# Keeping layer B's weighed sums with features on partitions, and spreading their denominators through memory

## The chip, the cores and the metric

The kernel runs on one core of a Trainium2 chip, in one launch. The metric is the device time of an execution in microseconds; the time of a kernel is the median of its executions.

## The reference, cut to what matters

Four layers, A, B, A, B, each with a residual, over x of 2048 x 640 with 32 heads of 20 features. Layer A is linear attention. Layer B cuts the sequence into four segments of 512 and adds, by a gate for each head, an exact attention inside the segment and a read of a memory of the segments before it:

```python
for s in range(N):
    qs, ks, vs = q[:, :, s], k[:, :, s], v[:, :, s]
    logits = jnp.einsum("bhqd,bhkd->bhqk", qs, ks) * scale + mask
    p = _softmax(logits, axis=-1)
    a_dot = jnp.einsum("bhqk,bhkd->bhqd", p, vs)
    pq = phi(qs)
    num = jnp.einsum("bhld,bhde->bhle", pq, M)
    den = jnp.einsum("bhld,bhd->bhl", pq, z)[..., None] + 1e-6
    a_mem = num / den
    o = g * a_mem + (1.0 - g) * a_dot
    outs.append(o)
    ...
return o @ wo
```

In segment 0 the memory is empty, so a_mem is 0 there. The change is in the division of the exact attention by the softmax's sum, and in what follows it up to the product with wo.

## The kernel before, in words

Two streams of work are woven into one program. `dense` makes the projections, layer A, the memory reads and the output products. `attention` makes layer B's exact attention in 64 groups: two layers, four segments, eight groups of four heads. `run` takes a step from whichever stream has the lower sum of estimated costs; a step of attention counts SLOT (2420 ns), and three steps (the three stretches of STRETCHES) make one round. TensorE (PE) executes in the order so written; the instructions of the other engines and of SP's queue are put in order by the framework's scheduler.

Three groups are in work in a round. The new group gets its queries and keys from memory by four transfers on SP (`stacks`; the tiles qs and ks). `row_max` multiplies queries by keys and takes each query's maximum on VectorE (DVE) in five portions. `split_max` makes two halves of the maxima (the tile m, L1022 and L1023), `max_rows` turns them on PE (L1031), copies them on ScalarE (ACT; the tile mt, L1033), and stores them by two SP transfers as two more rows of the queries (L1036). Then `scores` can multiply keys by queries with the maximum already taken off (L1048), ACT takes the exponential (L1052), GpSimd (POOL) masks it (L1059), and `weigh` multiplies it with the values (L1075). The values carry a column of ones, so PSUM holds, for each of four heads, 20 rows of weighed sums and one row of denominators, at 32 partitions a head, over 512 queries on the free dimension.

`evacuate` copies this to SBUF (oTf, L1081), with the denominator scaled by the gate. In the next stretch `normalize` turns it by four fp32 transposes on PE (L1088), so that tokens are on partitions; DVE takes the reciprocals of the denominators (L1091) and multiplies (L1098; L1095 in segment 0), and POOL adds the product to the memory's part, which lies in the tile otok (L1099). `b_memory` has written that part. `b_out` makes the output: for each tile of 128 tokens, five fp32 transposes back to features on partitions (`turn`, L319), a split in two fp16 halves by ACT (L323) and DVE (L324), and two half products with wo (`o_half`, L395), the residual by ACT and POOL (L476, L477).

In the first layer B, `b_out` of segment s - 2 is woven into the projections of segment s, and those of segments 2 and 3 into the next layer A. In the second, the four run at the end, beside the attention of segment 3, and segments 0 and 1 wait for that in memory (`b_spill`). SP's queue, in order, carries the loads of queries and keys, the stores of the projections (L859 to L863), the rows of the maxima, and the loads of x and of layer A's queries. PSUM is handed out in rotation, eight banks.

Of the kernel before, what the change touches and what calls it, by code (L numbers as in the profile page):

```python
# [142 lines left out]
class Kernel:  # L143
# [18 lines left out]
    def setup(self):  # L162
# [7 lines left out]
        self.g_last = cp.tile([P, D + 1], F32, name="g_last")  # L170
# [351 lines left out]
    def g_first(self, s, box, w, L, behind=None):  # L522
# [30 lines left out]
        def memory():  # L553
            if s == 0:
                L["v"] = [self.new_v(None) for _ in range(C - 1)]
                L["G"] = [v[:, :D + 1] for v in L["v"]] + [self.g_last]
# [308 lines left out]
    def b_project(self, st):  # L865
# [68 lines left out]
    def b_memory(self, st, mem):  # L934
        st["o"] = self.sb.tile([P, NT, D], F32, tag="big", name="otok", bufs=3)
        if st["s"] > 0:
            for i in range(NT):
# [4 lines left out]
    def b_spill(self, st):  # L942

        od = self.dr.tile([NT, P, D], F32, name="od%d" % st["s"])
        self.nc.sync.dma_start(od.rearrange("i p d -> p i d"), st["o"])
        st["od"], st["o"] = od, None
        yield 0.0

    def b_out(self, st, wo, src, dst, norm):

        yield lambda: st.get("attended")
# [4 lines left out]
        def turned(i):  # L956
            if st["o"] is not None:
                o = st["o"][:, i]
            else:
                o = self.row("ol")  # L960
                nc.sync.dma_start(o, st["od"][i])
            oT.append(self.new_oT())
            return self.turn(o, oT[i], 0)
# [3 lines left out]
        for i in range(NT):  # L967
# [3 lines left out]
            for n in range(2):  # L971
                yield from (c for c in [next(t, None)] if c)
                self.o_half(oT[i], wo, "B", x, xn, n, later=not st.get("ends"))
# [105 lines left out]
    def evacuate(self, G):  # L1079
        G["oT"] = self.bp.tile([P, 512], F32, tag="oTf", name="oTf", bufs=1)  # L1080
        self.nc.scalar.activation(G["oT"], G["pv"], AF.Copy, scale=self.cg[:, G["g"]:G["g"] + 1])  # L1081

    def normalize(self, G):
        nc, bp, sb, g, st = self.nc, self.bp, self.sb, G["g"], G["st"]
        oT = G["oT"]
# [4 lines left out]
        rc = sb.tile([P, NT, 4], F32, tag="rc4", name="rc4", bufs=2)  # L1090
        nc.vector.reciprocal(rc, pr[:, :, :, DH])  # L1091
        o = st["o"][:, :, 80 * g:80 * g + 80].rearrange("q i (h e) -> q i h e", h=4)
        rb = rc[:, :, :, None].to_broadcast([P, NT, 4, DH])
        if st["s"] == 0:
            nc.vector.tensor_tensor(o, pr[:, :, :, :DH], rb, op=OP.mult)  # L1095
        else:
            tmp = sb.tile([P, NT, 4, DH], F32, tag="er", name="tmp", bufs=3)
            nc.vector.tensor_tensor(tmp, pr[:, :, :, :DH], rb, op=OP.mult)  # L1098
# [264 lines left out]
```

## Time and profile before

| | |
|---|---|
| median of 3 executions | 1738.13 us (1735.6 to 1741.74) |
| the profiled execution | 1736.07 us, span 1734.4 us |
| granted TensorE clock | 0.998 |
| PE busy | 1666.1 us, 96% |
| DVE busy | 1180.9 us, 68% |
| ACT busy | 969.7 us, 56% |
| POOL busy | 517.7 us, 30% |
| moved by DMA | 187.58 MB, 108 GB/s on average |

The span is the time from the first to the last instruction of the profiled execution. An engine's busy time leaves out the issuing of transfers and waits on semaphores. A line of the groups reads: source line, engine, operation, out<-in by the program's tile names, shapes and count, then busy time in all and the mean of one in ns, then the idle time ahead of these instructions and what ended it. In the timeline the columns are start, duration, engine, line, operation. SPq is SP's queue issuing a transfer; its duration is the issue, not the transfer.

### The profile page before, as it was taken

What the parts mean: (1) busy time and instruction counts of PE and PEld (TensorE: products, weight loads), DVE (VectorE), ACT (ScalarE), POOL (GpSimd) and SP (SyncE); (2) the same over time, 40 slices, a digit from 0 to 9 for tenths busy, and PEclk for the clock granted to TensorE, in tenths of its full rate; (3) what the DMA queues carried; (4) which work ended last, traced back from release to release, by engine and by line L of the source; (5) the groups of instructions that cost most, each with busy time, mean ns of one, the idle gap of its engine ahead of it and who ended that gap; (6) DMA issues with size and microseconds to landing.
All of it is one profiled execution on the core that took longest, in us unless ns stands there. A gap on an engine that the chain in (4) does not pass through costs nothing.

```text
span 1734.4 us, 36014 instructions
## 1 busy us (share of the span) xinstructions
PE 1666.1 (96%) x13032; PEld 1047.5 (60%) x13032; DVE 1180.9 (68%) x3849; ACT 969.7 (56%) x1818; POOL 517.7 (30%) x982
## 2 busy tenths in 40 slices
PE   6999999999999999999999999999999999999998
PEld 4676667664565576556556777666546545645555
DVE  8645534577787677759864456746777877878773
ACT  5545433357557645667675544333665576666673
POOL 1543350012123312334351301221422432233452
PEclk9999999999999999999999999999999999999999
DMA  7522452422322322352211303423232323223432
GB/s 262 184 109 95 150 195 97 139 76 82 113 71 73 113 96 68 120 179 95 78 48 51 103 32 122 175 98 116 75 102 85 112 81 108 93 82 111 131 115 92
DMA packets 118330, 187.58 MB, mean 108 GB/s; under 512 B 13949, under 2 KB 79613, under 8 KB 115849
## 3 DMA queue, kind: packets, MB, share of 16 engines
q1 hardware_dynamic: 105896, 142.68, 25.5%
q0 software_dynamic: 3040, 21.63, 3.4%
q10 hardware_dynamic: 9216, 20.98, 3.1%
q8 instruction: 103, 1.69, 0.4%
q14 instruction: 75, 0.61, 0.1%
HBM read 106.05 MB, written 78.64 MB: 106 GB/s over the span
## 4 chain that ended last, share of the span: by engine, by line
PE 78%; DVE 10%; ACT 6%; issue 2%; POOL 2%; DMA 1%; SPq 1%; ACTq 0%; POOLq 0%; DVEq 0%
PE ps L395 32%; PE ps L381 17%; PE ps L1075 7%; PE ps L1048 4%; ACT pe L1052 3%; PE ps L1007 3%; PE ps L319 3%; PE ps L564 3%; PE ps L450 3%; DVE ps L1013 2%; PE ps L1088 1%; PE ps L891 1%; PE ps L730 1%; DVE st L338 1%; DVE xn L479 1%
## 5 line engine op out<-in xcount | busy, mean ns | idle before, releaser
L1013 DVE CUSTOM_DVE_ANT_0 ps<-ps,maskw 128x512 f32<-128x512 f32 (+3 forms) x1024 | 472.5, 519 | 38.0 <-PE ps L1007 35.7
L1052 ACT ACTIVATE pe<-ps,lsc 128x512 f32<-128x512 f32 x640 | 394.8, 696 | 87.6 <-PE ps L1048 84.9
L1059 POOL TENSOR_SCALAR_AFFINE_SELECT pe<-pe 128x256 f32<-128x256 f32 (+1 forms) x640 | 229.7, 365 | 449.2 <-ACT pe L1052 444.0
L395 PEld LDWEIGHTS <-xT 128*128 128x128 f16 x2880 | 280.3, 98 | 114.6 <-issue 9.3
L395 PEld LDWEIGHTS <-oT 128*128 128x128 f16 x1920 | 185.7, 98 | 80.5 <-issue 7.0
L1075 PE MATMUL ps<-pe,v 128*32 128x512 f32 (+3 forms) x2048 | 162.2, 436 | 11.5 <-POOL pe L1059 5.1
L395 PE MATMUL ps<-w_Bo,oT 128*128 128x320 f16 x960 | 142.3, 302 | 2.8 <-ACT pe L1052 1.1
L1013 DVE DVE_READ_ACCUMULATOR2_ANT mg<- 128x1 f32 x1024 | 143.9, 141 | 0.0
L381 PE MATMUL ps<-xT,w_Bq 128*128 128x512 f16 x600 | 140.2, 380 | 1.9 <-ACT pe L1052 0.8
L395 PE MATMUL ps<-w_Bv,xT 128*128 128x320 f16 x960 | 139.7, 300 | 0.8 <-DVE otok L1095 0.6
L381 PE MATMUL ps<-xT,w_Bk 128*128 128x512 f16 x600 | 138.8, 380 | 1.2 <-ACT pe L1052 1.2
L395 PE MATMUL ps<-w_Ak,xT 128*128 128x320 f16 x960 | 136.1, 300 | 0.0
L1007 PE MATMUL ps<-ks,qs 60*128 60x512 f16 (+3 forms) x1024 | 123.1, 298 | 6.7 <-ACT pe L1052 2.9
L856 DVE SCALAR_TENSOR_TENSOR nat<-ps,nat 128x512 f16<-128x512 f32 x80 | 55.2, 690 | 89.2 <-ACT nat L855 89.1
L1048 PE MATMUL ps<-qs,ks 62*128 62x512 f16 (+3 forms) x1024 | 105.9, 301 | 3.0 <-DMA qs<-mt 1.5
L1075 PEld LDWEIGHTS ps<-pe,v 128*32 128x32 f32 x2048 | 65.3, 109 | 71.9 <-issue 45.8
L421 POOL TENSOR_SCALAR e<-e 128x320 f32<-128x320 f32 (+1 forms) x52 | 82.9, 1594 | 82.4 <-ACT e L417 78.2
L855 ACT ACTIVATE nat<-ps 128x512 f16<-128x512 f32 x80 | 48.2, 603 | 91.8 <-PE ps L381 69.2
L381 PEld LDWEIGHTS <-w_Bk 128*128 128x128 f16 x600 | 57.3, 98 | 65.5 <-issue 5.6
L381 PEld LDWEIGHTS <-w_Bq 128*128 128x128 f16 x600 | 56.7, 98 | 65.9 <-issue 7.8
L1007 PEld LDWEIGHTS <-qs 60*128 60x128 f16 x1024 | 50.0, 94 | 70.9 <-issue 44.7
L343 POOL TENSOR_TENSOR rs<-rs,mhalf 128x1 f32<-128x1 f32 x48 | 27.0, 563 | 218.8 <-DVE rs L342 218.7
(217 smaller groups left out, 2630.7 us busy)
## 6 DMA issues: line engine op xcount, KB each, us to landing
x<-xn ACTq DMA_DIRECT2D x48, 320.0 KB
qs<-qd SPq DMA_DIRECT2D x128, 120.0 KB
ks<-kd SPq DMA_DIRECT2D x128, 120.0 KB
xo<-x SPq DMA_DIRECT2D x48, 320.0 KB
pqi<-pqd SPq DMA_DIRECT2D x32, 320.0 KB
qd<-nat SPq DMA_DIRECT2D x40, 256.0 KB
kd<-nat SPq DMA_DIRECT2D x40, 256.0 KB
x<-in_A_x SPq DMA_DIRECT2D x16, 320.0 KB
```

What stands on the lines that cost most here:

```text
L319: nc.tensor.transpose(pt[:, (c - c0) * P:(c - c0 + 1) * P], src[:, c * P:(c + 1) * P], self.ident)
L381: nc.tensor.matmul(p, w[:, c, a, t * P:(t + 1) * P], xT[:, c, b, :], start=k == 0, stop=k == 3 * C - 1)
L395: nc.tensor.matmul(p, xT[:, c, a, i * P:(i + 1) * P], w[:, c, b, n * HN:(n + 1) * HN], start=k == 0, stop=k == 3 * C - 1)
L421: nc.gpsimd.tensor_scalar(e, e, 1.0, eps, op0=OP.min, op1=OP.add)
L450: nc.tensor.matmul(nd[:, lo - k * cut:hi - k * cut], pq[t], mem[:, OFF[t] + lo - a:OFF[t] + hi - a], start=first, stop=True, skip_group_ch ...
L856: nc.vector.scalar_tensor_tensor(nat[:, 1], p, QK_SHIFT, nat[:, 0], op0=OP.mult, op1=OP.subtract)
L1007: nc.tensor.matmul(bs[par][:, a:a + n], qs[r, p, i * P:(i + 1) * P], ks[r, p, :n], start=True, stop=True)
L1013: nc.vector.tensor_tensor_reduce(bs[par][:, a:a + n], bs[par][:, a:a + n], self.maskw[:, SEG - n:], 1.0, NEG, OP.add, OP.max, G["mg"][:, p ...
L1048: nc.tensor.matmul(b[:, a:a + n], ks[r, p, j * P:(j + 1) * P], qs[r, p, j * P:], start=True, stop=True)
L1052: nc.scalar.activation(e, b, AF.Exp, scale=self.lsc)
L1059: nc.gpsimd.affine_select(d, d, pattern=pat, compare_op=OP.is_ge, fill=0.0, base=0, channel_multiplier=-1)
L1075: nc.tensor.matmul(G["pv"][32 * h4:32 * h4 + 32, j * P:], v[j][:, h * E1:h * E1 + 32], G.pop((p, par, j)), start=j == 0, stop=j == 2, skip ...
```

## The change

In all segments but the last of the second layer B, the weighed sums are not turned. `evacuate` stores the four rows of denominators to memory and loads them again, spread over 128 partitions x 16. `normalize` takes the reciprocals of these, stores them, loads each head's row 32 times over by four transfers (rb), multiplies oTf by rb in place on DVE, and packs the four heads' 20 rows each into od in memory, with features as rows, by four more transfers. Thus a group makes eleven more transfers, all on SP's queue. `merged` loads a tile of 128 tokens from od with features on partitions (ot). In segment 0 ACT and POOL split it at once; in the others PE turns the memory's part, DVE adds the two, and ACT and POOL split the sum. The last segment of the second layer B keeps the old way (`normalize_direct`). An output may start one round later than before (`packed` for `attended`).

```diff
-        self.g_last = cp.tile([P, D + 1], F32, name="g_last")
...
+                last = sb.tile([P, MW], F32, tag="mem", name="g_last", bufs=2)
+                L["G"] = [v[:, :D + 1] for v in L["v"] + [last]]
...
+        st["od"] = self.dr.tile([D, SEG], F32, tag="od", name="od", bufs=NSEG)
...
+    def merged(self, st, i, dst):
+        nc = self.nc
+        ot = self.row("ot").rearrange("p (c t) -> p c t", c=C)
+        nc.sync.dma_start(ot, st["od"].rearrange("(c p) t -> p c t", p=P)[:, :, i * P:(i + 1) * P])
+        if st["s"] == 0:
+            nc.scalar.activation(dst[:, :, 0], ot, AF.Copy)
+            nc.gpsimd.tensor_tensor(dst[:, :, 1], ot, dst[:, :, 0], op=OP.subtract)
+            return
+        if st["o"] is not None:
+            o = st["o"][:, i]
+        else:
+            o = self.row("ol")
+            nc.sync.dma_start(o, st["am"][i])
+        for c0, c1 in ((0, 3), (3, 5)):
+            pt = self.bank()
+            n = c1 - c0
+            for c in range(c0, c1):
+                nc.tensor.transpose(pt[:, (c - c0) * P:(c - c0 + 1) * P], o[:, c * P:(c + 1) * P], self.ident)
+            v = ot[:, c0:c1]
+            nc.vector.tensor_tensor(v, pt[:, :n * P].rearrange("p (c t) -> p c t", c=n), v, op=OP.add)
+            nc.scalar.activation(dst[:, c0:c1, 0], v, AF.Copy)
+            nc.gpsimd.tensor_tensor(dst[:, c0:c1, 1], v, dst[:, c0:c1, 0], op=OP.subtract)
+            yield n * 110.0
...
     def b_out(self, st, wo, src, dst, norm):
-        yield lambda: st.get("attended")
+        yield lambda: st.get("packed")
...
             oT.append(self.new_oT())
-            return self.turn(o, oT[i], 0)
+            return self.turn(st["o"][:, i], oT[i], 0) if st["direct"] else self.merged(st, i, oT[i])
...
     def evacuate(self, G):
-        G["oT"] = self.bp.tile([P, 512], F32, tag="oTf", name="oTf", bufs=1)
-        self.nc.scalar.activation(G["oT"], G["pv"], AF.Copy, scale=self.cg[:, G["g"]:G["g"] + 1])
+        nc, bp = self.nc, self.bp
+        G["oT"] = bp.tile([P, SEG], F32, tag="oTf", name="oTf", bufs=2)
+        nc.scalar.activation(G["oT"], G["pv"], AF.Copy, scale=self.cg[:, G["g"]:G["g"] + 1])
+        if G["g"] == NG - 1:
+            G["st"]["attended"] = True
+        if G["st"]["direct"]:
+            return
+        den = self.dr.tile([4, SEG], F32, tag="den", name="den", bufs=2)
+        nc.sync.dma_start(den, G["oT"][DH::32])
+        G["rd"] = bp.tile([P, 16], F32, tag="rd", name="rd", bufs=2)
+        nc.sync.dma_start(G["rd"], den.rearrange("h (q t) -> (h q) t", t=16))
 
     def normalize(self, G):
+        if G["st"]["direct"]:
+            return self.normalize_direct(G)
+        nc, g, st, oT, rd = self.nc, G["g"], G["st"], G["oT"], G["rd"]
+        nc.vector.reciprocal(rd, rd)
+        rden = self.dr.tile([4, SEG], F32, tag="rden", name="rden", bufs=2)
+        nc.sync.dma_start(rden.rearrange("h (q t) -> (h q) t", t=16), rd)
+        rb = self.sb.tile([P, SEG], F32, tag="er", name="rb", bufs=3)
+        for h in range(4):
+            nc.sync.dma_start(rb[32 * h:32 * h + 32], rden[h:h + 1].to_broadcast([32, SEG]))
+        nc.vector.tensor_tensor(oT, oT, rb, op=OP.mult)
+        for h in range(4):
+            r = 80 * g + DH * h
+            nc.sync.dma_start(st["od"][r:r + DH], oT[32 * h:32 * h + DH])
...
     def attention(self, segs):
...
+            if done and done["g"] == NG - 1:
+                done["st"]["packed"] = True
+            done = None if old and old["st"]["direct"] else old
             old, prev = prev, new
...
-            segs = [dict(s=s, w=wB, v=[], pq=[], acc=acc) for s in range(NSEG)]
+            segs = [dict(s=s, w=wB, v=[], pq=[], acc=acc, direct=last and s == NSEG - 1) for s in range(NSEG)]
...
-                    aux = chain(aux, when(segs[s - 2], "attended", late))
+                    aux = chain(aux, when(segs[s - 2], "remembered" if last else "packed", late))
```

How the instructions stand now, at two places. First SP's queue in the first layer B, segment 2, from one group's rows of maxima (qs<-mt) to the next group's; before:

```order
L1036 DMA qs<-mt 2x8x128 x2
L993 DMA qs<-qd 60x2x512 x2
L993 DMA ks_2752<-kd 60x2x512 x2
L330 DMA xo<-x_87 128x640
L1036 DMA qs<-mt 2x8x128 x2
```

and now, from the denominators of one group to the second row transfer of the next maxima (den, rd, rden and rb are the denominators and their reciprocals on their way, od the packed heads):

```order
L1111 DMA den<-oTf 4x512
L1016 DMA qs<-qd 60x2x512 x2
L1016 DMA ks_2751<-kd 60x2x512
L1113 DMA rd<-den 128x16
L1016 DMA ks_2751<-kd 60x2x512
L329 DMA xo<-x_86 128x640
L956 DMA ot<-od 128x5x128
L1123 DMA rden<-rd 128x16
L1126 DMA rb<-rden 32x512 x4
L1059 DMA qs<-mt 2x8x128
L1130 DMA od<-oTf 20x512 x4
L1059 DMA qs<-mt 2x8x128
```

The four packing transfers stand between the two row transfers of the next maxima. They stand so in 17 of the 56 changed groups; in 18 both row transfers come ahead of them, in 19 both come after, and in the last two of the first layer B no rows follow.

Then DVE at the same place. Before, the reciprocal and the product follow at once on PE's transposes, ahead of the rest of the maxima (L1013, printed as ISA, each with its readout):

```order
L1091 RECIPROCAL rc_8682<-ps 128x16
L1098 TENSOR_TENSOR tmp<-ps,rc_8682 128x320
L1013 ISA ps,mg<-ps,maskw 128x384
L1013 ISA mg 128x1
L1013 ISA ps,mg<-ps,maskw 128x384
```

and now the product stands after the split of the next group's maxima (L1045, L1046) and three of the maxima after that (L1036 here):

```order
L1045 TENSOR_SCALAR m_8893<-mg 128x2x8
L1046 SCALAR_TENSOR_TENSOR m_8893<-mg,m_8893 128x2x8
L1036 ISA ps,mg<-ps,maskw 128x512
L1036 ISA mg 128x1
L1036 ISA ps,mg<-ps,maskw 128x512
L1036 ISA mg 128x1
L1036 ISA ps,mg<-ps,maskw 128x384
L1036 ISA mg 128x1
L1127 TENSOR_TENSOR oTf<-oTf,rb 128x512
```

The product has moved from ahead of the split of the next maxima to behind it; the reciprocal (L1121) now stands thirteen rows ahead of the split.

More of the change, by code (lines that the diff above doesn't have):

```diff
@@ L934, in b_memory @@
     def b_memory(self, st, mem):
-        st["o"] = self.sb.tile([P, NT, D], F32, tag="big", name="otok", bufs=3)
         if st["s"] > 0:
+            st["o"] = self.sb.tile([P, NT, D], F32, tag="big", name="otok", bufs=3)
             for i in range(NT):
@@ L972, in b_out @@
                 yield from (c for c in [next(t, None)] if c)
-                self.o_half(oT[i], wo, "B", x, xn, n, later=not st.get("ends"))
+                self.o_half(oT[i], wo, "B", x, xn, n, later=not st["direct"])
                 yield self.COST_N
@@ L1127, in attention @@
                         continue
+                    if op == "out" and G["st"]["direct"] and not G["st"].get("remembered"):
+                        yield lambda: G["st"].get("remembered")
                     if op == "max":
```

43 lines of the change are left out of this document (15 added, 28 removed).

## The prediction

> **What bounds the kernel now.** The page first: busy shares, their course over the span, then the chain that ended last.
>
> ```profile
> PE 1666.1 (96%) x13032; PEld 1047.5 (60%) x13032; DVE 1180.9 (68%) x3849; ACT 969.7 (56%) x1818; POOL 517.7 (30%) x982
> ...
> PE   6999999999999999999999999999999999999998
> ...
> PE 78%; DVE 10%; ACT 6%; issue 2%; POOL 2%; DMA 1%; SPq 1%; ACTq 0%; POOLq 0%; DVEq 0%
> ```
>
> TensorE is busy for 1666.1 of 1734.4 us and in every slice but the first, so its work is the time: what is taken from it is won, and what makes it wait is lost, almost one for one. Next the lists of waits, first SP's queue, then PE.
>
> ```profile
> SPq L1036 <- ACT mt L1033: 435.3, 61, 21.1
> ```
>
> ```profile
> PE ps L1048 <- DMA qs<-mt: 1.5, 1, 1.5
> ```
>
> SP, whose queue gets the new transfers, mostly stands waiting for the next group's maxima (435.3 us). PE waits only once for the transfer that puts these into the queries' stack (1.5 us). Both can change. One group in the dense part of layer B, by the timeline:
>
> ```profile
> 690.32 1.28 SPq L1036 DMA_DIRECT2D qs<-mt  x2
> ...
> 691.33 0.69 ACT L1081 ACTIVATE oTf<-ps,cg 128x512 f32<-128x512 f32 x1 [1.03 <-PE ps L1075]
> 691.71 0.81 SPq L993 DMA_DIRECT2D qs<-qd  x2
> ...
> 693.72 0.49 PEld L1088 LDWEIGHTS ps<-ident,oTf 128*128 128x128 f32 x4
> 693.85 0.60 PE L1088 MATMUL ps<-ident,oTf 128*128 128x128 f32 x4
> ...
> 694.38 0.61 PE L1048 MATMUL ps<-qs,ks 62*128 62x512 f16 x4
> ...
> 701.34 0.16 DVE L1023 SCALAR_TENSOR_TENSOR m<-mg,m 128x16 f16<-128x16 f32 x1
> ...
> 702.84 0.27 ACT L1033 ACTIVATE mt<-pm 32x128 f16<-32x128 f16 x1 [0.25 <-PE pm L1031]
> 703.13 1.29 SPq L1036 DMA_DIRECT2D qs<-mt  x2
> ```
>
> A group takes 703.13 - 690.32 = 12.8 us. In it the weighed sums leave PSUM by 691.33 + 0.69 = 692.02 (the copy), the next group's maxima are split by 701.34 + 0.16 = 701.50, and their two row transfers start at 703.13. The first scores that need such rows (L1048) start 694.38 - 690.32 = 4.06 us after the first row transfer.
>
> **The change part by part.** The groups of instructions that carry the terms:
>
> ```profile
> L1088 PE MATMUL ps<-ident,oTf 128*128 128x128 f32 x256 | 38.4, 273 | 0.0
> ...
> L319 PE MATMUL ps<-ident,ol 128*128 128x128 f32 x40 | 7.4, 290 | 1.9 <-ACT pe L1052 1.9
> ...
> L1098 DVE TENSOR_TENSOR tmp<-ps,rc 128x320 f32<-128x320 f32 x48 | 23.4, 488 | 1.8
> ...
> L1091 DVE RECIPROCAL rc<-ps 128x16 f32<-128x16 f32 x64 | 16.3, 254 | 48.6 <-PE ps L1088 48.3
> ...
> L424 DVE SCALAR_TENSOR_TENSOR pkT<-e,r 128x512 f32<-128x512 f32 x30 | 20.7, 690 | 16.1 <-ACT r L419 15.5
> ...
> L324 DVE TENSOR_TENSOR oT<-ps,oT 128x384 f16<-128x384 f32 (+1 forms) x128 | 61.3, 486 | 31.8 <-ACT oT L323 31.4
> ...
> L1099 POOL TENSOR_TENSOR otok<-otok,tmp 128x320 f32<-128x320 f32 x47 | 41.2, 876 | 93.8 <-DVE tmp L1098 93.8
> ...
> L1013 DVE CUSTOM_DVE_ANT_0 ps<-ps,maskw 128x512 f32<-128x512 f32 (+3 forms) x1024 | 472.5, 519 | 38.0 <-PE ps L1007 35.7
> ...
> L1013 DVE DVE_READ_ACCUMULATOR2_ANT mg<- 128x1 f32 x1024 | 143.9, 141 | 0.0
> ```
>
> *Removed from PE.* 56 of 64 groups lose their four transposes: 224 x (38.4 / 256 = 0.150) = 33.6 us. Segment 0 of both layers loses the turning of its four token tiles, 2 x 4 x 5 = 40 transposes at 7.4 / 40 = 0.185: 7.4 us. Segments 1 to 3 of the first layer B, and 1 and 2 of the second, still turn the memory's part, so nothing goes there. Together 41.0 us. The lower bound is the share in which PE is the chain, 0.78 x 41.0 = 32.0, since DVE or ACT ends last in the rest. I take the middle, 36.
>
> *DVE.* Per group it had 0.254 + 0.488 and now has 0.254 + 0.690 (the product over 128 x 512, priced by L424, both operands in SBUF): 0.20 more, 11 us in 56 groups. In the output step 28 tiles lose two subtractions of 0.486 (27 us), and 20 tiles get two additions of that size (19 us). Net +3 us, of which the chain's 10% counts: under 1 us.
>
> *POOL and ACT.* POOL loses 40 additions of 0.876 (35 us) and gets 28 tiles' subtractions over 640 columns, by the same rate 1.75 us each (49 us): +14 us on an engine that is busy 30%. What matters is that the last step before the output product is now a POOL instruction, longer than DVE's 0.486, behind the masks and residual additions in POOL's queue. The next tile is turned one tile ahead, so two half products and attention's work cover it, but the first tile of a segment has no such lead. I allow 3 us, between 0 and, if eight tiles each wait 1.75 longer, 14. ACT's copies change by under 1 us.
>
> *SP.* Each of 56 groups adds 2 + 1 + 4 + 4 = 11 transfers, and the tiles add 28 loads of `ot`. At the 0.81 / 2 = 0.40 us that a queries' load takes there, that is 644 x 0.40 = 258 us of issuing, less than the 435.3 us above. The count alone costs nothing, but the order does: SP runs in order, and five waits per group now stand in it. What one trip through memory costs, two places of the timeline where SP waited for a store before it could load:
>
> ```profile
> 299.10 0.38 SPq L859 DMA_DIRECT2D qd<-nat  x1
> 301.65 0.35 SPq L993 DMA_DIRECT2D qs<-qd  x1
> ```
>
> ```profile
> 309.73 0.34 SPq L862 DMA_DIRECT2D kd<-nat  x1
> ...
> 311.84 0.34 SPq L993 DMA_DIRECT2D ks<-kd  x1
> ```
>
> So 301.65 - 299.10 = 2.55 and 311.84 - 309.73 = 2.11 us from issue to issue, for 256 KB stores. The upper end is in the chain of waits:
>
> ```profile
> 658.43 3.82 DMA ks<-kd
> ...
> 703.13 5.26 DMA qs<-mt
> ```
>
> I take 2.2 per trip, near the shorter one, because 8 KB move here, and keep 2.1 and 3.8 for the range. The Trainium skill ("DMA: Bandwidth & Descriptors", Anatomy of one DMA) gives about 2.0 us of fixed cost per transfer, and its Rules for kernel authors say that under 64 KB one pays mostly overhead: a rule against this change. The two places above agree in size; with 2.0 in place of 2.2 the path below is 0.8 us shorter.
>
> From the copy's end: denominators out 2.2, back in 2.2, reciprocal 0.25, out 2.2, four repeating loads (three issues of 0.40 ahead of the last, then 2.2): 10.25 us until the product may start. DVE comes to it, by the order rows of the change, three maxima after the split: 701.50 - 692.02 = 9.48, and 3 x (0.519 + 0.141) = 1.98, so 11.46 us after the copy. PE reaches that point 0.53 us earlier without its transposes (694.38 - 693.85), leaving 10.93. So the product runs in its turn, with 0.7 us to spare, and DVE, with the next maxima queued behind it, does not stand; from trips of 2.4 us on it does.
>
> But of 56 groups, 17 have the four packing transfers between the two row transfers of the next maxima, as the order rows show. They wait for the product: 1.98 + 0.69 = 2.67 us after the split, and take 4 x 0.40 = 1.6. The second row transfer starts 4.27 after the split, where it started 703.13 + 0.64 - 701.50 = 2.27 before: 2.0 us later. Behind it on SP stand the next denominators and stacks, and PE's L1048 waits for its landing. Its slack in the shown group: 4.06 - 0.64 - 2.2 = 1.22, less the 0.53 of the removed transposes, 0.7. So PE stands 2.0 - 0.7 = 1.3 us: 17 x 1.3 = 22 us. Bounds: 0 (slack larger than 2 us) and 17 x 2.0 = 34 (none). In 18 groups both row transfers come ahead of the packing, and nothing waits. In 19 both come after it; there the product stands ahead of the split or at a segment's end, and I charge 0.2 us each, 4 us, with 0 and 19 x 1.6 = 30 as ends.
>
> *Without a price.* The repeated reciprocals hold one of three buffers that the feature maps share, which may hold up an exponential on ACT: nothing to 5 us, inside the range. Outputs start a group later; other projections fill PE then. The last segment keeps its path, so the tail does not move.
>
> **Sum.** -36 + 1 + 3 + 22 + 4 = -6 us. The profiled execution took 1736.07 us, 1.7 over its span and 2.1 under the median of 1738.13; against the median this gives 1732 us. A measurement of this kernel can tell about 0.3%, some 5 us, from no change, so the likeliest case is a small gain at the edge of what can be seen. Its own range: 41 won, 0.5 lost in each of the 17 and 0.1 in each of the 19 (-41 + 4 + 8.5 + 2 = -26), to 32 won, 1.7 lost in each of the 17 and 0.7 in each of the 19 (-32 + 4 + 29 + 13 = +14): 1712 to 1752.
>
> **Rivals.**
>
> *The waits are hidden.* PE has over 2 us of other work between the rows and their use in most of the 17 groups, and they cost nothing. For it: PE's wait for the rows is 1.5 us in all now. Against it: that one wait came at an undelayed transfer. Then -41 + 1 + 3 = -37 to -30: about 1704 us.
>
> *SP's queue becomes the bound (slower).* If a trip takes 2.8 us under the load of the dense stretches, the product may start at 4 x 2.8 + 0.25 + 1.2 = 12.65 after the copy, 1.7 us past DVE's turn for it. DVE stands with the maxima behind it, SP with the row transfers, and PE with the scores; it decides from 2.4 us on. For it: the 3.82 and 5.26 us above, both in this kernel, and the 2.55. Against it: those are 2 pieces of a whole chain in which DMA has 1%. Price: 17 split groups and about half of the 19, 26 x 1.7 = 44 us on top: 1732 + 44 = 1776, and 1752 where only 12 groups are hit so.
>
> *Saving and loss cancel.* The slack is used up everywhere (as at 703.13, where the rows came too late already), the 17 groups lose 2.0 each, 34 us, against 36: -36 + 1 + 3 + 34 = 2, about 1740 us.
>
> **How the numbers follow.** Forecast 0.40, hidden waits 0.24, SP as bound 0.26, cancelling 0.10. Of the forecast's range of 1712 to 1752, 0.52 lies below 1733, 0.25 within 0.3% of the median and 0.23 above. Faster: 0.24 + 0.52 x 0.40 = 0.45. Same: 0.25 x 0.40 + 0.5 x 0.10 = 0.15. Slower: 0.26 + 0.23 x 0.40 + 0.5 x 0.10 = 0.40. For 8 in 10 the range leaves out the better half of the hidden case and a third of the slower one: 1703 to 1772.
>
> **What would show it.** Right: L1088's group falls to 32 transposes and 4.8 us, PE's busy time by about 41 us; PE's wait for qs<-mt grows from 1.5 to some 20 us, in the split groups; SP's wait for mt shrinks and waits for the product (oTf) appear in its list. Hidden waits: PE's wait for qs<-mt stays under 5 us. SP as bound: DVE shows idle time ahead of the product released by rb's transfers, more than 1 us a time, and PE's share falls below 94%. The forecast is wrong if PE waits for something that is not in the chain from the product to the rows, such as oT from POOL or a buffer held by rb.

## The result, and the profile after

The changed kernel takes 1821.21 us (median of 4 runs, 1815.55 to 1822.84), the kernel before 1739.49 beside it: a ratio of 1.0466, with an interval of 1.0436 to 1.0497. It is 82 us slower, where 1732 was forecast and 1703 to 1772 given. The busy shares and the chain of the page, then the granted clock of the profiled execution:

```profile
PE 1685.3 (93%) x12768; PEld 1028.4 (56%) x12768; DVE 1181.6 (65%) x3833; ACT 970.5 (53%) x1810; POOL 531.2 (29%) x990
...
PE 63%; DVE 12%; DMA 9%; ACT 6%; issue 4%; POOL 3%; SPq 3%; ACTq 0%; DVEq 0%; POOLq 0%
```

```profile
core 0: 1821.1 us, clock 0.977
```

TensorE executes 264 matmuls fewer, and its line of the groups for the transposes fell as forecast (L1136 is the changed kernel's L1088):

```profile
L1136 PE MATMUL ps<-ident,oTf 128*128 128x128 f32 x32 | 4.9, 277 | 0.9 <-ACT oTf L1105 0.8
```

Still it is busy 19.2 us longer (1685.3 against 1666.1), and not busy for 1821.1 - 1685.3 = 135.8 us, 67.5 more than before (1734.4 - 1666.1 = 68.3). The two make the 86.7 us by which the span grew. The list of PE's waits names what it stands for, SP's list what SP stands for (waiting instruction, what released it, total, times, longest):

```profile
PE ps L1071 <- DMA qs<-mt: 20.2, 19, 2.6
PE ps L318 <- ACT xh L367: 14.6, 6, 7.3
PE ps L1030 <- DMA ks<-kd: 11.3, 10, 2.4
PE ps L449 <- DMA pqi<-pqd: 10.0, 3, 5.3
```

```profile
SPq L1059 <- ACT mt L1056: 195.8, 48, 13.8
...
SPq L1130 <- DVE oTf L1127: 66.9, 33, 6.1
SPq L1126 <- DMA rden<-rd: 52.6, 41, 3.3
SPq L1123 <- DVE rd L1121: 52.5, 28, 4.2
```

Three of PE's four are loads that SP issues: the rows of the maxima, the stacks, and layer A's queries. With the loads of the memory's part (ol, 5.5 us) PE's waits for loads come to 47.0 us, where they were 1.5. SP's wait for the maxima fell from 435.3 to 195.8 us; the chain of the denominators took its place. One group of the dense part, by the timeline:

```profile
707.27 1.40 SPq L1130 DMA_DIRECT2D od<-oTf  x4
707.37 0.69 ACT L1105 ACTIVATE oTf<-ps,cg 128x512 f32<-128x512 f32 x1 [0.97 <-PE ps L1098]
708.71 0.63 SPq L1059 DMA_DIRECT2D qs<-mt  x1
709.45 0.54 SPq L1111 DMA_DIRECT2D den<-oTf  x1
...
711.52 0.35 SPq L1113 DMA_DIRECT2D rd<-den  x1
...
713.63 0.25 DVE L1121 RECIPROCAL rd<-rd 128x16 f32<-128x16 f32 x1 [0.89 <-DMA rd<-den]
...
713.91 0.33 SPq L1123 DMA_DIRECT2D rden<-rd  x1
716.56 1.72 SPq L1126 DMA_DIRECT2D rb<-rden  x4
...
719.66 0.66 SPq L1059 DMA_DIRECT2D qs<-mt  x1
...
721.88 0.69 DVE L1127 TENSOR_TENSOR oTf<-oTf,rb 128x512 f32<-128x512 f32 x1 [1.96 <-DMA rb<-rden]
722.60 2.26 SPq L1130 DMA_DIRECT2D od<-oTf  x4
...
724.90 0.62 SPq L1059 DMA_DIRECT2D qs<-mt  x1
...
726.70 0.60 PE L1071 MATMUL ps<-qs,ks 62*128 62x512 f16 x3 [1.68 <-DMA qs<-mt]
```

The product starts 721.88 - (707.37 + 0.69) = 13.82 us after the copy's end, and the packing stands between the two row transfers: the second starts 724.90 - 719.66 = 5.24 us after the first, where it was 0.64 before. PE then waits 1.68 us for it. This is the forecast's split group, but a long one: over the 17 split groups of this trace the second row transfer starts 2.81 us after the first at the median. Of PE's 20.2 us for the rows 15.8 stand in split groups, under a quarter of the 67.5 us that it stands longer.

### The profile page after: what moved, and what is told of

It is laid out like the page before. It is cut to its first block, busy times and chain, and to the rows that moved or that the text cites. A ratio compares the mean times of both kernels' runs of the same rounds, so it can differ in the third digit from the quotient of the medians.

```text
span 1821.1 us, 36523 instructions
## 1 busy us (share of the span) xinstructions
PE 1685.3 (93%) x12768; PEld 1028.4 (56%) x12768; DVE 1181.6 (65%) x3833; ACT 970.5 (53%) x1810; POOL 531.2 (29%) x990
## 4 chain that ended last, share of the span: by engine, by line
PE 63%; DVE 12%; DMA 9%; ACT 6%; issue 4%; POOL 3%; SPq 3%; ACTq 0%; DVEq 0%; POOLq 0%
PE ps L394 27%; PE ps L380 13%; PE ps L1098 6%; DVE ps L1036 3%; PE ps L1071 3%; PE ps L449 3%; PE ps L1030 3%; PE ps L564 3%; ACT pe L1075 3%; PE ps L318 2%; DMA rd<-den 2%; PE ps L892 1%; DMA rden<-rd 1%; DMA qs<-mt 1%; PE ps L730 1%
## 5 line engine op out<-in xcount | busy, mean ns | idle before, releaser
L1036 DVE CUSTOM_DVE_ANT_0 ps<-ps,maskw 128x128 f32<-128x128 f32 (+3 forms) x1024 | 473.5, 517 | 100.0 <-PE ps L1030 97.5
L1082 POOL TENSOR_SCALAR_AFFINE_SELECT pe<-pe 128x256 f32<-128x256 f32 (+1 forms) x640 | 233.4, 370 | 570.0 <-ACT pe L1075 565.1
L394 PEld LDWEIGHTS <-oT 128*128 128x128 f16 x1920 | 188.2, 99 | 87.7 <-issue 12.7
L1098 PE MATMUL ps<-pe,v 128*32 128x512 f32 (+3 forms) x2048 | 173.7, 456 | 20.0 <-POOL pe L1082 5.8
L1030 PE MATMUL ps<-ks,qs 60*128 60x128 f16 (+3 forms) x1024 | 130.9, 303 | 25.7 <-DMA ks<-kd 11.3
L394 PE MATMUL ps<-w_Bo,oT 128*128 128x320 f16 x960 | 148.3, 310 | 6.4 <-DVE mg L1036 3.6
L1036 DVE DVE_READ_ACCUMULATOR2_ANT mg<- 128x1 f32 x1024 | 142.8, 139 | 0.0
L1071 PE MATMUL ps<-qs,ks 62*128 62x128 f16 (+3 forms) x1024 | 116.5, 306 | 21.4 <-DMA qs<-mt 20.2
```

Of the source, the lines that this page charges most:

```text
L394: nc.tensor.matmul(p, xT[:, c, a, i * P:(i + 1) * P], w[:, c, b, n * HN:(n + 1) * HN], start=k == 0, stop=k == 3 * C - 1)
L1030: nc.tensor.matmul(bs[par][:, a:a + n], qs[r, p, i * P:(i + 1) * P], ks[r, p, :n], start=True, stop=True)
L1036: nc.vector.tensor_tensor_reduce(bs[par][:, a:a + n], bs[par][:, a:a + n], self.maskw[:, SEG - n:], 1.0, NEG, OP.add, OP.max, G["mg"][:, p ...
L1071: nc.tensor.matmul(b[:, a:a + n], ks[r, p, j * P:(j + 1) * P], qs[r, p, j * P:], start=True, stop=True)
L1082: nc.gpsimd.affine_select(d, d, pattern=pat, compare_op=OP.is_ge, fill=0.0, base=0, channel_multiplier=-1)
L1098: nc.tensor.matmul(G["pv"][32 * h4:32 * h4 + 32, j * P:], v[j][:, h * E1:h * E1 + 32], G.pop((p, par, j)), start=j == 0, stop=j == 2, skip ...
```

## The experiments

All ratios are to the kernel before, run beside them. Three theories stood at the start: SP's queue holds up what PE needs (Q), the trips are longer than assumed and DVE stands for them (L), or the number of transfers costs (N). Later expectations split these: W is the part of Q that waits for trips, I the part that only issues, B the bytes, D the work of DVE, O the output step.

**Which queue the rows stand in.** The rows of the maxima are issued from ACT (e1), the stacks too (e2); the control is the kernel before with e1's edit (e10).

```diff
-QUEUES = ('gpsimd', 'scalar', 'sync', 'sync', 'gpsimd', 'sync')
+QUEUES = ('gpsimd', 'scalar', 'sync', 'scalar', 'gpsimd', 'sync')   # e1, e2, e10
-                nc.sync.dma_start(tl[64 * par:64 * par + 60],
+                nc.scalar.dma_start(tl[64 * par:64 * par + 60],     # e2
```

> The changed kernel, but the two row transfers of the maxima (qs<-mt) are issued from ACT's queue, where they are made, and no longer stand among the eleven on SP. Theory Q (SP works in order, and what PE needs next stands behind the new chain): PE's idle time ahead of the first scores (20 us by the gaps in front of L1071) goes, with some of the half clock that follows it: 1785 to 1800 against 1821. Theory L (the trips through memory are too long, and DVE stands at reciprocal and product): DVE stands as before, 1815 to 1825. Theory N (644 more transfers slow all others down by their number): 1815 to 1825.

> As the run before, and the loads of queries and keys (qs<-qd, ks<-kd) go to ACT's queue too: 384 issues of 0.4 to 0.6 us, some 170 us more on ACT, which is busy 53%. Theory Q: the idle time ahead of L1030 (22 us) goes as well, 1750 to 1775, unless ACT's own queue becomes what PE waits for. L and N: 1815 or slower.

> The kernel before with only the row transfers of the maxima issued from ACT in place of SP: the control for the run of the changed kernel with that edit (1774). If the rows were late on SP before too, it is faster than before, 1725 to 1735 us; if they only became late by the chain (theory Q), it is within 5 us of before, or some us slower, since each issue takes ACT about 0.6 us of its queue: 1735 to 1745.

Measured: e1 1773.56 us, 1.0209 (1.0188 to 1.0231); e2 1798.32, 1.0341 (1.0324 to 1.0358); e10 1747.27, 1.0049 (1.0033 to 1.0065). Taking the rows off SP gives back 48 us of the 82, although the same edit costs the kernel before 8 us. So most of the loss has to do with what stands in SP's queue. PE's wait for the rows falls to 11.0 us in e1, and the stacks leave its list. But the stacks on ACT as well are worse again, which Q did not expect.

**PE's transposes put back in the changed kernel (e4),** unread:

```diff
         nc, g, st, oT, rd = self.nc, G["g"], G["st"], G["oT"], G["rd"]
+        pt = self.bank()
+        for i in range(NT):
+            nc.tensor.transpose(pt[:, i * P:(i + 1) * P], oT[:, i * P:(i + 1) * P], self.ident)
```

> The changed kernel, with the four transposes of each group put back on PE, their result unread: 224 x 0.15 = 34 us of PE work. If PE were still what sets the time: 1855. If PE stands for SP anyway (Q or L), the transposes partly fill the time in which it stands and keep its clock up: 1815 to 1835.

Measured: 1816.25 us, 1.0453 (1.0425 to 1.0481), no different from the changed kernel. The transposes cost nothing there, so PE's work alone no longer sets the time. Part of their price is won back: with them the runs' granted clock is 0.982 to 0.988, without them 0.976 to 0.979, and PE's wait for the rows is 11.5 us in place of 20.2.

**Constants in place of the trips (e3, f1).** The loads of the spread and of rb read a constant; in e3 it is stored when layer B opens, in f1 at the start. Both leave out the division.

```diff
-        nc.sync.dma_start(G["rd"], den.rearrange("h (q t) -> (h q) t", t=16))
+        nc.sync.dma_start(G["rd"], self.cden.rearrange("h (q t) -> (h q) t", t=16))
-        nc.sync.dma_start(rden.rearrange("h (q t) -> (h q) t", t=16), rd)
+        nc.sync.dma_start(rden.rearrange("h (q t) -> (h q) t", t=16), self.crd)
-            nc.sync.dma_start(rb[32 * h:32 * h + 32], rden[h:h + 1].to_broadcast([32, SEG]))
+            nc.sync.dma_start(rb[32 * h:32 * h + 32], self.cden[h:h + 1].to_broadcast([32, SEG]))
```

> The changed kernel with all eleven transfers and both DVE instructions, but the loads come from a constant in memory and the reciprocals' store from a constant tile, so that inside the chain only the copy and the product are waited for. It leaves out the division (sums are multiplied by a constant). Q and L: the waits are the loss, so most of the 82 us and part of PE's 41 us are back: 1700 to 1740. N: the number is the loss, and it is unchanged: 1800 to 1821.

> As the earlier run without trip waits, but with the constants stored at the very start of the kernel by GpSimd, so that nothing is held up before the first group: all eleven transfers of a group stay, with the same shapes, but the loads of the spread and of the repeated denominators read a constant that was stored long before, and the store takes a constant too, so that none of them waits for another transfer. It leaves out the division. Known: without the seven transfers and the trips 1736. If the waits inside the chain make the loss (SP stands in order for each trip), this is 1740 to 1760; if the count of transfers on SP makes it, 1795 to 1820; half and half 1770 to 1785.

Measured: e3 1806.05, 1.0391 (1.0372 to 1.041); f1 1799.87, 1.0359 (1.0337 to 1.0381). Neither settles it. Freed from their data, the loads were put elsewhere in SP's queue by the scheduler, some far ahead, where they stood for buffers; and DVE still waited for the loads.

**Fewer trips (e9).** One transfer repeats the undivided denominators, and DVE takes the reciprocals of the whole tile; the rows are on ACT.

```diff
-        nc.vector.reciprocal(rd, rd)
...
-        for h in range(4):
-            nc.sync.dma_start(rb[32 * h:32 * h + 32], rden[h:h + 1].to_broadcast([32, SEG]))
+        src = bass.AP(tensor=rden.tensor, offset=rden.offset, ap=[[SEG, 4], [0, 32], [1, SEG]])
+        nc.sync.dma_start(rb, src)
+        nc.vector.reciprocal(rb, rb)
```

> The changed kernel with two trips in place of four (denominators stored, then one transfer that repeats each row 32 times, the reciprocal on DVE over the whole 128 x 512 tile, the product), six transfers a group in place of eleven, and the row transfers of the maxima issued from ACT in place of SP. Theory Q: what stays behind the chain is halved as well, so 1735 to 1760 us against 1774 with the rows on ACT alone. Theory O (output step): no more than the rows gained, 1765 to 1780. The longer reciprocal costs DVE 56 times 0.4 us, 25 us, which counts at most by DVE's 12% of the chain, 3 us.

Measured: 2003.23 us, 1.1514 (1.1486 to 1.1541), largely because of one instruction: it adds 3352 - 247 ns to a group's reciprocal, 3.1 us, where 0.4 was expected, and 56 x 3.1 = 174 us of the 230 by which e9 is slower than e1:

```profile
L1123 DVE RECIPROCAL rb<-rb 128x512 f32<-128x512 f32 x56 | 187.7, 3352 | 105.2 <-DMA rb<-den 105.1
```

The run tells nothing of the trips. It shows why the change spreads the denominators first.

**The chain alone, and the outputs alone (e11, e12).** e11 adds the eleven transfers, the reciprocal and the product to the kernel before; e12 takes the seven transfers and the trips out of the changed one.

```diff
+        # e11, in the kernel before: evacuate and normalize of the change beside the old path
+            nc.sync.dma_start(st["od2"][r:r + DH], oT[32 * h:32 * h + DH])
-        # e12, in the changed kernel: den, rd, rden and rb are gone
-        nc.vector.tensor_tensor(oT, oT, rb, op=OP.mult)
+        nc.vector.tensor_scalar(oT, oT, 2.0 ** -14, None, op0=OP.mult)
```

> The kernel before, with the whole path of the division added beside the old one: denominators stored, spread, inverted, stored, repeated, the product, and the four packing transfers, whose result nobody reads. The transposes, the adding on POOL and the output step stay those of before. If SP's order makes the loss (theory Q: what PE needs stands behind the chain's transfers), the chain alone brings it: 82 us of loss over before, with the transposes kept on a PE that then stands anyway, so 1800 to 1825 us (the changed kernel with transposes kept took 1816). If the output step makes it (theory O: loads of ot, POOL's subtraction as the last step, outputs a group later), the time is near before: 1740 to 1760. Half and half (first layer B by the output step, second by the rows on SP): about 1770 to 1785.

> The changed kernel without its way through memory for the denominators: no den, rd, rden and rb; the weighed sums are multiplied by a constant on DVE and packed by the same four transfers, and the output step is the changed one. It leaves out the division. Seven of eleven transfers a group and all four trips are gone. If SP's chain makes the loss (theory Q), this is near or under before: 1700 to 1745 us. If the output step makes it (theory O), most of the loss stays: 1790 to 1820. Half and half: about 1760 to 1775.

Measured: e11 1788.16, 1.0287 (1.027 to 1.0304); e12 1735.59, 0.998 (0.9968 to 0.9992). Without the seven transfers and their trips (e12) the whole loss is gone. Beside the old path, and with the packing (e11), they cost 49 us, which lies between the cases that were expected. And without them, and without dividing, the change would win 3.5 us: there was hardly anything to gain.

**The trips spread over later stretches (f2, f4, f5).** The same computation and the same eleven transfers, cut into steps at other places of the round. In f4 the repeating loads stand behind the rows. In f5 all of it stands behind the rows and, but for the second store and the packing, behind the next stacks, over three rounds.

```diff
+    def spread(self, G): ...      # rd <- den
+    def invert(self, G): ...      # reciprocal, rden <- rd
+    def repeat(self, G): ...      # rb <- rden, four loads
+    def product(self, G): ...
+    def pack(self, G): ...
+                            with self.tc.issue_after(self.rowed.ins):    # f4: repeat; f5: invert, pack
+                            with self.tc.issue_after(self.stacked.ins):  # f5: store, repeat
```

> The same spreading over two rounds, but without holding the transfers behind the rows and the exponentials: the scheduler then puts the load of the spread right behind the store of the denominators again (or one packing transfer between them), and the packing ahead of it. So the trips overlap with nothing more on SP than in the changed kernel, except for the repeating loads and the product, which come a round later. If SP standing for trips makes the loss, this lies between: 1765 to 1800 us, clearly above the held form. If the place in the program alone matters and not the order on SP, it equals the held form.

> The changed kernel with the same eleven transfers and four trips, but spread over two rounds: after the copy only the denominators' store; the load of the spread after the next stretch's second exponential; the reciprocal and its store at the end of the round; the four repeating loads in the next round, held behind the row transfers of the maxima; the product and the packing after that. The row transfers always come first. If the loss is SP standing for trips with what PE needs behind it, each trip now has other work in front of its wait: 1735 to 1755 us, and PE's waits for qs<-mt and ks<-kd fall from 20.2 and 11.3 to under 5 each. If the number of transfers or the load on the memory makes the loss, it stays at 1790 to 1820. If later outputs (one stretch later than in the changed kernel) matter, somewhere between with PE's waits for xh and pqi the longest.

> The changed kernel's computation in full, its eleven transfers spread over three rounds so that each stands behind what PE needs: behind the row transfers the inverted denominators' store and the packing of two groups earlier, then the stacks, and behind the stacks the denominators' store, the four repeating loads and the load of the spread. Every trip has some 4 to 9 us of other work before it is waited for. Theory W: 1740 to 1760, and PE's waits for qs<-mt and ks<-kd (20.2 and 11.3) under 5 each. Theory N: 1795 to 1820. An output starts one round later still, which may cost up to 15 us in the first layer B, so W allows 1740 to 1770.

Measured: f2 1812.39, 1.0424 (1.0396 to 1.0453); f4 1884.57, 1.0843 (1.0816 to 1.087); f5 1801.64, 1.0355 (1.0326 to 1.0385). In f4 the load of the spread, the packing and the reciprocals' store still stood ahead of the last stack. PE's waits in f4, then in f5:

```profile
PE ps L1030 <- DMA ks<-kd: 88.6, 35, 5.5
...
PE ps L1071 <- DMA qs<-mt: 1.5, 1, 1.5
```

```profile
PE ps L1030 <- DMA ks<-kd: 4.4, 1, 4.4
PE ps L1071 <- DMA qs<-mt: 3.6, 4, 1.9
```

f4 frees the rows (20.2 to 1.5 us) and puts the whole wait on the stacks (11.3 to 88.6): whoever stands behind the chain pays. f5 frees both, and still loses 63 us. Covered trips alone do not mend it. All three runs lie above what their expectations gave for a loss by waits.

**The chain on GpSimd's queue (e5).** All eleven transfers are issued by `nc.gpsimd` in place of `nc.sync`.

> The changed kernel with all eleven transfers of the chain issued from GpSimd's queue in place of SP's. Theory W: PE's waits for qs<-mt, ks<-kd and pqi go back to those of before (under 5 us each), but POOL now stands for the trips with the masks behind it, so PE waits for pe instead; 1750 to 1800, and POOL's masks in PE's list of waits with 20 us or more. Theory N, if it is the traffic: no change, 1800 to 1820, and the waits for qs<-mt and ks<-kd stay.

Measured: 1862.91, 1.0707 (1.0662 to 1.0751). PE hardly waits for the rows (0.9 us) and no longer for the stacks, but for the masks, as expected; the price was higher than expected:

```profile
PE ps L1098 <- POOL pe L1082: 29.5, 23, 2.6
```

**Number, bytes, place, and DVE's work (f6, f7, g1, g2, g3).** f7 is e12 with a second pass on DVE. f6 adds the seven transfers, held behind the denominators' store, with nobody reading what they bring. g1 shrinks them. g2 puts them, full-size, behind the next stacks. g3 is e12 with the transposes back. All five leave out the division.

```diff
+        with self.tc.issue_after(G["cp"].ins):      # f6: behind the store of den
+            nc.sync.dma_start(G["rd"], self.cden.rearrange("h (q t) -> (h q) t", t=16))
...
+                nc.sync.dma_start(rb[32 * h:32 * h + 32], self.cden[h:h + 1].to_broadcast([32, SEG]))
+                nc.sync.dma_start(rb[32 * h:32 * h + 32, :16], self.cden[h:h + 1, :16].to_broadcast([32, 16]))  # g1
+        with self.tc.issue_after(self.stacked.ins):  # g2: all seven, at the end of a round
+            nc.tensor.transpose(pt[:, i * P:(i + 1) * P], oT[:, i * P:(i + 1) * P], self.ident)  # g3
```

> All eleven transfers of a group, in one bunch behind the denominators' store on SP, which stands behind the row transfers: the spread and the repeated rows are loaded from a constant, nobody reads them, and the second store takes a constant, so that SP waits for no trip. DVE multiplies by a constant in two passes (2 x 0.43 us, about the 0.25 + 0.69 of the changed kernel). It leaves out the division. Theory W (SP standing in order for the trips): 1740 to 1760, since only issue time is added, 7 x 0.35 = 2.5 us a group of some 13. Theory N (the number of transfers and their traffic): 1795 to 1820. Theory D (DVE's product): 1760 to 1775, as in the run with DVE's work alone.

> The kernel without the seven transfers (1736) with DVE multiplying by a constant in two passes in place of one: 56 x 0.43 = 24 us more work on DVE and nothing else. It leaves out the division. Theories W and N: within 5 us of 1736. Theory D (DVE's longer work between the copy and the packing, and ahead of the next maxima): 1755 to 1770.

> The run with all transfers in one fixed place and no data waited for (1815), with the seven transfers shrunk: 4 x 16 elements for the three small ones and 32 x 16 for each repeating load, in the same number and the same order on SP, 24 KB in place of 280 KB in a group. It leaves out the division. Theory I (issue time on SP and the place ahead of the stacks): 1800 to 1815. Theory B (bytes and packets on the memory's side): 1740 to 1755. Both in part: about 1775.

> The same seven full-size transfers, in the same number, with nobody waiting for their data, but at the end of a round, behind the stacks of the next group; the packing stays where it is in the run with DVE's work alone (1740). It leaves out the division. Theory I: what PE needs is ahead of them, so 1740 to 1760, with PE's wait for ks<-kd under 8 us (33.9 in the run with the bunch ahead). Theory B: 1795 to 1815, wherever they stand. What of I remains is the projections' stores and the loads of x behind them, up to 20 us more.

> The kernel without the seven transfers (1736) with each group's four transposes put back on PE, unread: 224 x 0.150 = 34 us of work. It leaves out the division. If PE's work is the time, as the prediction had it: 1765 to 1772. If the transposes fill time in which PE stands for others anyway, as they did in the changed kernel (1816 against 1821): 1733 to 1745.

| kernel | us | ratio to before (interval) |
|---|---|---|
| g3: new outputs and packing, transposes kept | 1754.1 | 1.0092 (1.0077 to 1.0107) |
| e12: the same without the transposes | 1735.59 | 0.998 (0.9968 to 0.9992) |
| f7: and DVE's second pass | 1739.96 | 1.0006 (0.9997 to 1.0016) |
| g2: and the seven transfers, behind the stacks | 1775.97 | 1.0209 (1.0188 to 1.0229) |
| g1: seven tiny ones in place of these, ahead of the stacks | 1809.74 | 1.041 (1.0385 to 1.0434) |
| f6: full-size ones, ahead of the stacks | 1815.35 | 1.0441 (1.0419 to 1.0462) |
| the changed kernel | 1821.21 | 1.0466 (1.0436 to 1.0497) |

Seven transfers with hardly any bytes, for whose data nobody waits, cost 70 us (g1 against f7). Bytes add nothing that the intervals tell apart (f6). Nor are f6 and the changed kernel clearly apart, so a loss of this size needs no wait for a trip; but f6 has another order on SP, and what the waits cost in the changed kernel's own order is not shown. About half of the 70 is the transfers' place: behind the stacks, full-size, they cost 36. What place means, by SP's queue in the timeline, first f7, then g1:

```profile
699.91 1.28 SPq L1059 DMA_DIRECT2D qs<-mt  x2
701.29 0.83 SPq L1016 DMA_DIRECT2D qs<-qd  x2
702.17 1.68 SPq L1016 DMA_DIRECT2D ks<-kd  x2
```

```profile
700.32 1.32 SPq L1063 DMA_DIRECT2D qs<-mt  x2
701.98 0.54 SPq L1115 DMA_DIRECT2D den<-oTf  x1
702.56 0.46 SPq L1118 DMA_DIRECT2D rd<-cden  x1
703.07 0.29 SPq L1128 DMA_DIRECT2D rden<-crd  x1
703.40 1.69 SPq L1132 DMA_DIRECT2D rb<-cden  x4
705.32 1.40 SPq L1137 DMA_DIRECT2D od<-oTf  x4
706.82 0.79 SPq L1020 DMA_DIRECT2D qs<-qd  x2
```

The next stacks start 1.38 us after the rows in f7 and 6.50 in g1: seven issues of 0.29 to 0.54 us, 2.98 in all, then the packing and the gaps between them. The group of f7 shown is a short one: over all groups the last of the four stack loads is issued 5.4 us after the end of the rows at the median in f7, where the packing mostly stands among the stacks, and 8.4 in g1. PE's wait for the stacks in f7, in g1 and in g2, from their lists of waits:

```profile
PE ps L449 <- DMA pqi<-pqd: 4.3, 3, 3.1
PE ps L1030 <- DMA ks<-kd: 4.0, 5, 1.7
```

```profile
PE ps L1034 <- DMA ks<-kd: 36.0, 27, 4.4
```

```profile
PE ps L453 <- DMA pqi<-pqd: 12.7, 3, 6.6
PE ps L1034 <- DMA ks<-kd: 12.0, 7, 4.2
```

The pages of f7 and then g1 give PE's share of the 70:

```profile
PE 1652.7 (95%) x12768; PEld 1019.1 (59%) x12768; DVE 1177.8 (68%) x3833; ACT 968.2 (56%) x1810; POOL 525.7 (30%) x990
PE 1682.0 (93%) x12768; PEld 1026.3 (57%) x12768; DVE 1186.5 (66%) x3833; ACT 971.0 (54%) x1810; POOL 532.6 (29%) x992
```

The span grows by 1806.4 - 1738.1 = 68.3 us. PE stands 39.0 of it, 32.0 for the stacks (36.0 against 4.0), and is busy 29.3 longer with the same matmuls. The granted clock fell from 0.992 to 0.977, an estimate of 0.023 x 1806.4 - 0.008 x 1738.1 = 28 us of clock not granted. So some 60 of the 68 us are the stacks' delay and the clock that falls with it. The buffers that the repeated rows share with the feature maps show no part in it: in the lists of g1 no exponential waits for rb, and SP waits 1.2 us in all to issue it.

The stacks lead to the next maxima, and these to the next rows, so a delay there can come round again with each group. The remaining 36 us of g2 are only partly settled. Its profiled execution, the slowest of its four, is 46.7 us longer than that of f7: PE is busy 11.3 longer (1664.0 against 1652.7) and stands 35.4 longer, 17.8 for loads (pqi, queued on SP as well, 12.7 against 4.3), 11.4 for ACT and 8.7 for DVE. What delays ACT and DVE there, and what the 63 us of f5 consist of, is open. No run beat the kernel before by more than e12, which does not divide.

## Why the prediction was wrong, by its own steps

*Removed from PE: forecast -36, measured -18.5.* Between g3 and e12 the 34 us of transposes are worth 1754.1 - 1735.59 = 18.5 us, a little over half, so the lower bound of 0.78 was still too high; in the changed kernel itself they are worth nothing (e4). It is the price that was wrong: the line of the transposes is busy for 33.6 us in g3 too, but PE as a whole is busy only 1671.7 - 1651.4 = 20.3 us longer than in e12, because the records of the transposes overlap those of other matmuls (without them g3's PE records cover 1651.1 us). Of these 20.3 the 18.5 are "almost one for one".

*DVE +1 and outputs +3.* DVE's added pass costs 4.4 us (f7 against e12). The new output step with its packing, net of segment 0's turning, costs 16 us (g3, 1.0092); in g3 PE's wait for xh is 15.1 us, where it was 8.1:

```profile
PE ps L318 <- ACT xh L367: 15.1, 6, 7.9
```

It is 7.8 in e11, which keeps the old outputs. "Other projections fill PE then" was priced at nothing and is part of these 16.

*"The count alone costs nothing": forecast 0, measured 36 to 70.* This is the step that failed: with no data waited for, seven more transfers a group cost 36 us behind the stacks (g2) and 70 ahead of them (g1). It compared 258 us of issuing with 435.3 us in which SP waits, two sums over the kernel. But SP's idle time lies at the end of a group, ahead of the next maxima, and the issues stand at its start, ahead of the stacks. The stacks were said to stand behind the split, but only the row transfers got a price. The changed kernel's own order is a mixed one, in which PE waits 20.2 us for the rows, 11.3 for the stacks and 10.0 for pqi; how its 82 us divide between issuing and trips is not shown.

*The split groups: forecast +22.* PE's wait for qs<-mt is 20.2 us over 19 times, as foreseen (some 20, 17 groups). The rows' shift behind it was right too: 2.81 - 0.64 = 2.2 us at the median of the split groups, against 2.0 (the group shown, with 5.24 - 0.64 = 4.6, is one of the two longest). The chain was priced too short: 13.82 us in the group shown and 14.4 at the median of the 56, against 10.25. The trips themselves were about right: 711.52 - 709.45 = 2.07 and 716.56 - 713.91 = 2.65 us from issue to issue, 2.09 and 1.69 at the median, against 2.2. The section of the Trainium skill that the prediction drew on ("DMA: Bandwidth & Descriptors", Anatomy of one DMA) has its 2.0 us for transfers issued from GpSimd, and these are issued from SP. Missing from the chain were the denominators' store, which SP issues 709.45 - 708.06 = 1.39 us after the copy because packing and the second row stand ahead, and the repeating loads, 721.88 - 716.56 = 5.32 from the first issue to the product against 3.4.

*The rivals.* Slower won, but not by its mechanism. Its own signs were half there: PE's share fell below 94% (93%), but DVE's idle time ahead of the product is small; it stands at the reciprocal, ahead of it in the chain, 32 us in all:

```profile
L1127 DVE TENSOR_TENSOR oTf<-oTf,rb 128x512 f32<-128x512 f32 x56 | 41.3, 737 | 7.6 <-DMA rb<-rden 7.0 <-DMA qs<-mt 0.5
...
L1121 DVE RECIPROCAL rd<-rd 128x16 f32<-128x16 f32 x56 | 13.9, 247 | 32.2 <-DMA rd<-den 32.0
```

Its trips of 2.8 us were not the rule, and with no trip waited for a loss as large stands (f6). "The forecast is wrong if PE waits for something that is not in the chain" is what happened: stacks, pqi and xh.

*What no step had: the clock.* From 0.998 to 0.977 of full rate, an estimate from the two spans is 0.023 x 1821.1 - 0.002 x 1734.4 = 38 us of clock not granted; the trace has 85.4 us at half rate, where it had 6.8. PE's busy time agrees: the same 12768 matmuls take it 1685.3 - 1651.4 = 33.9 us longer than in e12, whose clock is 0.991.

## What to carry to other kernels

An in-order queue is priced by what stands behind each instruction in its stretch, not by its idle sum: here seven issues of some 0.4 us a group, ahead of the loads that start the next group, cost 70 us on a queue that waits for 200 to 400, some 28 of them by the clock that fell when PE stood. Before moving work off the busiest engine, take it out alone and see what is won: the transposes were worth half of their line's busy time, and without the new path's price the whole change could win only 3.5 us. When a wait is removed by an order or a queue, look at who stands behind instead; the rows' wait went to the stacks, and on another queue to the masks.

## What was not expected of the hardware

*The clock falls after PE has stood for half of a window.* In the clock's record of the changed kernel 15 stretches at half rate last 3.41 us and five 6.83. Windows of 3.41 us on their grid, each pair one after the other; the columns are length, PE, PEld, DVE, ACT and POOL busy, the granted clock, DMA share and GB/s:

```profile
739.09:742.50 3.41, 1.38 (x6) 0.39 (x4) 1.81 (x6) 0.69 (x1) 0.29 (x1) 1.00 0.23 58
742.50:745.91 3.41, 2.87 (x12) 1.36 (x13) 1.37 (x6) 1.84 (x3) 0.88 (x3) 0.50 0.49 149
```

```profile
858.53:861.94 3.41, 1.81 (x17) 0.46 (x19) 3.35 (x12) 2.65 (x6) 2.07 (x3) 1.00 0.34 109
861.94:865.35 3.41, 3.41 (x29) 1.48 (x21) 3.16 (x13) 0.95 (x2) 0.00 (x0) 0.50 0.23 55
1548.02:1551.43 3.41, 1.89 (x22) 1.05 (x24) 2.14 (x7) 2.07 (x4) 0.61 (x2) 1.00 0.01 2
1551.43:1554.84 3.41, 3.41 (x42) 1.68 (x43) 3.05 (x14) 1.65 (x4) 0.75 (x2) 1.00 0.01 1
872.18:875.59 3.41, 1.64 (x17) 0.86 (x15) 0.07 (x2) 0.00 (x0) 0.00 (x0) 1.00 1.02 280
875.59:879.00 3.41, 1.31 (x10) 0.87 (x10) 1.70 (x6) 2.51 (x6) 1.32 (x2) 1.00 0.34 85
```

After a window with PE busy 1.38 or 1.81 us the next is granted half the rate; after one with 1.89 it is not, and not after one with 1.64 either, so the border is not sharp. Of all windows at full rate in this trace, half rate followed 16 of the 19 in which PE stood for 1.8 us or more, 4 of the 8 with 1.5 to 1.8, and none of the others. A wait of 2 us can thus cost its own length and, at half rate, an estimated 0.5 x 3.41 = 1.7 us of the next window. The Trainium skill ("TensorE: Matmul & The Clock Gate", Why this matters for your kernels) asks for no idle gaps over about 3 us between matmuls. Here 3.41 - 1.81 = 1.60 us of standing in one window was enough, and the measurement decides.

*The reciprocal goes by the element.* On DVE 128x16 takes 0.25 us and 128x512 3.35 us (e9): 6.3 ns for each further element of a partition, where the product of that size takes 0.74 us in all.
